# K loads two heads ahead of V instead of three, and one output turn ahead of the last values, in a decode attention kernel

## The chip, the cores and the metric

The kernel runs on one core of a Trainium2 chip. The metric is the device time of one execution in microseconds (us). Each comparison takes executions of both kernels on the same chip, in rounds; all runs of this study were in the fast state. A program on one core can only be called slow against its own fastest run, and none was more than 1.5% above that. Executions of one kernel still differ by up to 1.5%, and part of what follows is about why. Of the experiments, e1 to e4 ran on one chip and e5 to e12 on another; the kernel before was run beside each, with medians of 211.78 us (e1 to e4), 211.69 us (e5 to e8) and 211.52 us (e9 to e12).

## The reference, cut to what matters

One decode step: attention of 4 rows over the last 2048 positions of a K and V cache with 16 K/V heads (two query heads each), plus a mixing step and an MLP on the same input. The code is shortened.

```python
W = min(4096, max(256, Sk // 4))                    # 2048
q = (x @ wq) ...                                    # 32 query heads of 128
k = jnp.repeat(k_cache[:, :, Sk - W:, :], rep, axis=1)
v = jnp.repeat(v_cache[:, :, Sk - W:, :], rep, axis=1)
p = softmax(einsum("bhqd,bhkd->bhqk", q, k) * Dh ** -0.5)
A = einsum("bhqk,bhkd->bhqd", p, v) ... @ wo
# B: x1 + gelu(layernorm(x1) @ w3) @ w4, with x1 = x + mixer(...)
out = x + A + B          # A and B both get xn = layernorm(x)
```

Per head that is 2 MB of K and 2 MB of V; with the weights 87.17 MB are read.

## The kernel before: the parts that matter

Loads are issued in program order by SyncE, into a pool of six K/V tiles; a load waits until a tile has been freed.

```python
kvp = ctx.enter_context(tc.tile_pool(name="kv", bufs=NKV))        # NKV = 6
...
order = [("K", 0), ("K", 1), ("K", 2)]
for h in range(Hkv):
    order.append(("V", h))
    if h + 3 < Hkv:
        order.append(("K", h + 3))
...                       # w4, in six pieces, comes after the last K/V tile
```

The main loop has one turn per head. In turn t TensorE does the scores of head t and the values of head t-2, in four steps; VectorE transposes the K tile of head t in four pieces, one step ahead, and does the softmax maxima of head t-1 between them. A turn with a number (turn 15) is such a pass of the loop; "head 14's turn", "the moved turn" and `o_turn` mean something else, the transposes that turn the output of a head.

```python
for t in range(Hkv):
    hm, hv, hf, hp = t - 1, t - 2, t - 3, t - 4
    for s in range(NSL):
        ...
        n = t * NSL + s + 1
        if n < Hkv * NSL:
            k_transpose(*divmod(n, NSL))     # VectorE, needs the K tile
        if s == 0:
            if hm >= 0:
                sm_max(hm)                   # VectorE: max of the scores, then dm
            ...
        elif s == 1 and hm >= 0:
            sm_maxT(hm)                      # TensorE, needs dm ("the max matmul", mg)
        ...
        if hv >= 0:
            pv(hv, s)                        # TensorE, needs the V tile
        k_scores(t, s)                       # TensorE, needs the transposed K
        ...
```

After the loop comes the drain: the softmax of head 15, the values of heads 14 and 15, the turn of their outputs (four transposes on TensorE), then the w4 matmuls and the last projection.

```python
sm_exp(hl)                 # hl = 15, on ScalarE
...
sm_turn(hl); sm_den(hl); sm_rec(hl)
o_scale(hl - 1)            # ScalarE
for s in range(NSL):
    pv(hl, s)              # 16 value matmuls of head 15
o_scale(hl)                # ScalarE
o_turn(hl - 1); o_sum(hl - 1)
...
o_turn(hl); o_sum(hl); o_spread(hl); o_pick(hl)
mlp_out(*pieces[0])        # first w4 matmuls
o_proj(hl)
mlp_out(*pieces[1]) ...    # up to the pieces that land last
```

Of the kernel before, what the change touches and what calls it, by code (L numbers as in the profile page):

```python
# [22 lines left out]
def kernel(  # L23
# [17 lines left out]
    _, Hkv, Sk, Dh = A_k_cache.shape  # L41
# [337 lines left out]
    def sm_rec(h):  # L379
        rd = small.tile([P, 1], F32, tag="rd", bufs=4)  # L380
        nc.vector.reciprocal(out=rd[:], in_=st.pop(("dn", h))[:])
        st["rd", h] = rd

    def pv(h, s):
        if s == 0:
            O_ps[h] = ps_o.tile([P, NSL, Dh], F32, tag="O", name="O")
        vn = kv_tiles["V", h][:].rearrange("p (s c) d -> p s c d", s=NSL)
        for g in range(NQD):
            c = s * NQD + g
            nc.tensor.matmul(out=O_ps[h][g * QD:(g + 1) * QD], lhsT=PT[h][:, c, :], rhs=vn[:, :, c, :],  # L390
                             start=(s == 0), stop=False, skip_group_check=True)
        if s == NSL - 1:
            PT.pop(h)

    def o_scale(h):
        O_sb[h] = bigp.tile([P, NSL, Dh], F32, tag="big", name="O_sb")
        nc.scalar.activation(out=O_sb[h][:], in_=O_ps.pop(h)[:], func=ACT.Copy, scale=st.pop(("rd", h))[:, 0:1])  # L397

    def o_turn(h):
        oT = ps_m.tile([P, NSL, P], F32, tag="m", name="oT")  # L400
        o = O_sb.pop(h)
        for s in range(NSL):
            nc.tensor.transpose(out=oT[:, s, :], in_=o[:, s, :], identity=ident_w[:, s * NJ:s * NJ + P])  # L403
        st["oT", h] = oT

    def o_sum(h):
        oT = st.pop(("oT", h))
        v = oT[:].rearrange("p s (g x) -> p (s g) x", g=NQD)[:, :, 0:NJ].rearrange("p g (b r) -> p b r g", r=rep)
        k = h % WOQ
        if k == 0:  # L410
            st["on"] = small.tile([P, WOH, B], BF16, tag="on", name="on")
        with nc.allow_low_precision("summed in float32"):
            nc.vector.reduce_sum(out=st["on"][:, k * rep:(k + 1) * rep, :].rearrange("p r b -> p b r"),  # L413
                                 in_=v, axis=AX.X)
# [73 lines left out]
            acc_matmuls([(gT[:, u, :], w4[:, u, :]) for u in range(i, min(i + 2, hi))])  # L488


    order = [("K", 0), ("K", 1), ("K", 2)]
    for h in range(Hkv):
        order.append(("V", h))
        if h + 3 < Hkv:
            order.append(("K", h + 3))
    W3_AFTER = ("V", 2)
    pos = {"n": 0, "free": NKV}

# [70 lines left out]
    hl = Hkv - 1  # L569
# [14 lines left out]
    sm_den(hl)  # L584
    sm_rec(hl)
    o_scale(hl - 1)
    for s in range(NSL):
        pv(hl, s)
    o_scale(hl)
    o_turn(hl - 1)  # L590
    o_sum(hl - 1)
    pieces = list(zip(W4_PIECES, W4_PIECES[1:]))
    acc_odd = ps_acc.tile([P, CW], F32, tag="g", name="acc_odd")
    second += [acc_odd, True]
# [50 lines left out]
```

## Time and profile before

| | before |
|---|---|
| median of 3 runs | 211.63 us (211.63 to 212.5) |
| span in the profile | 209.8 us |
| read | 87.17 MB, 97.5% of 16 DMA engines' time |
| TensorE, VectorE busy | 71%, 57% |
| TensorE's waits for V | 37.1 us, ten times |

In the views PE is TensorE, PEld its weight loads, DVE VectorE, ACT ScalarE and SP SyncE. Of the tiles, kn and vn are K and V as loaded, kt the transposed K, S the scores, mg the max matmul's result, O the values, O_sb the scaled output and oT the turned one.

TensorE's waits for V are one line in the list of waits (engine and line, releaser: us in total, times, longest):

```profile
PE O L390 <- DMA vn<-in_A_v_cache_dram: 37.1, 10, 14.0
```

The rows of 40 slices tell which engine is never free: the DMA row is at 9 nearly throughout, TensorE's is not. The prediction below shows those lines. One row that it does not show matters later, TensorE's granted clock, the share of its full speed that it was allowed, in tenths (page of the kernel before):

```profile
PEclk9999589696969556958999979997999985969999
```

Here the reader sees that the clock falls to about half in single slices all over the run, also in the slice that covers 183.6 to 188.8 us (the 36th, a 6).

### The profile page before, as it was taken

To read this page: it belongs to the slowest core of one execution; us is meant where nothing else is said; L and a number is where in the kernel's file an instruction comes from. 1 tells how busy PE (TensorE), PEld (TensorE's weight loads), DVE (VectorE), ACT (ScalarE), POOL (GpSimd) and SP (SyncE) were. 2 spreads that over 40 slices of the span, in tenths; PEclk is the share of its full clock that TensorE was granted. 3 is DMA by queue.
4 is the path that set the end of the run, shared out by engine and by line. 5 is a ranking of instruction groups with operands and counts; after the bars stand their busy time and mean duration, and the time that the engine had idled before them with its cause. 6 is when DMAs were issued, how large, how long until landed. Compare 5 with 4: busy or idle time off the path is not lost.

```text
span 209.8 us, 2403 instructions
## 1 busy us (share of the span) xinstructions
PE 149.9 (71%) x955; PEld 62.8 (30%) x955; DVE 120.4 (57%) x217; ACT 33.9 (16%) x64; POOL 2.8 (1%) x15
## 2 busy tenths in 40 slices
PE   0287496869694009659899599977994926989884
PEld 0133132223231003214364143332532401425362
DVE  3741899584831082816706869995299471771421
ACT  7602201020211000202102121120111110202300
POOL 4010000000000000000000000000000000000000
PEclk9999589696969556958999979997999985969999
DMA  7999999999999999999999999999999999999991
GB/s 301 400 412 437 428 428 428 436 422 428 469 408 420 433 428 427 438 431 428 431 437 428 422 425 446 425 425 436 422 436 428 421 435 440 425 425 448 418 402 72
DMA packets 6659, 87.32 MB, mean 416 GB/s; under 512 B 748, under 2 KB 1016, under 8 KB 1656
## 3 DMA queue, kind: packets, MB, share of 16 engines
q1 hardware_dynamic: 6640, 87.17, 97.5%
q8 instruction: 7, 0.11, 0.2%
q14 instruction: 4, 0.03, 0.0%
q10 hardware_dynamic: 8, 0.00, 0.0%
HBM read 87.17 MB, written 0.00 MB: 415 GB/s over the span
## 4 chain that ended last, share of the span: by engine, by line
DMA 72%; PE 18%; DVE 6%; ACT 1%; issue 1%; SPq 0%; DVEq 0%
DMA vn<-in_A_v_cache_dram 35%; DMA w_sb<-in_B_w_dram 31%; PE S L338 7%; DMA wq_sb<-in_A_wq_dram 6%; DVE kt L225 3%; PE acc L183 2%; PE g_ps L456 2%; PE q_ps L285 2%; PE O L390 2%; PE oT L403 1%; DVE qz L317 1%; PE gT_ps L468 1%; DVE mx L344 1%; PE S L360 1%; ACT q_sb L296 1%
## 5 line engine op out<-in xcount | busy, mean ns | idle before, releaser
L225 DVE STREAM_TRANSPOSE kt<-kn 128x1024 int32<-128x1024 int32 x64 | 76.4, 1217 | 10.9 <-DMA kn<-in_A_k_cache_dram 10.6
L338 PE MATMUL S<-kt,qz 128*128 128x512 bf16 x256 | 79.7, 441 | 3.1 <-DVE kt L225 3.1
L390 PE MATMUL O<-vn,PT 128*32 128x512 bf16 x256 | 27.4, 426 | 38.9 <-DMA vn<-in_A_v_cache_dram 37.1
L338 PEld LDWEIGHTS <-qz 128*128 128x128 bf16 x256 | 21.7, 104 | 41.5 <-issue 25.8
L366 ACT ACTIVATE E<-S 128x512 bf16<-128x512 f32 x16 | 9.5, 597 | 122.6 <-PE S L360 122.6
L390 PEld LDWEIGHTS <-PT 128*32 128x32 bf16 x256 | 7.2, 94 | 47.3 <-issue 30.2
L372 DVE STREAM_TRANSPOSE PT<-E 128x512 bf16<-128x512 bf16 x16 | 11.4, 710 | 14.9 <-ACT E L366 14.9
L356 DVE TENSOR_REDUCE nm<-mg 8x1 bf16<-8x16 f32 x16 | 2.4, 152 | 20.7 <-PE mg L351 20.7
L397 ACT ACTIVATE O_sb<-O,rd 128x512 f32<-128x512 f32 x16 | 11.0, 686 | 15.6 <-issue 11.0
L413 DVE TENSOR_REDUCE on<-oT 128x8 bf16<-128x128 f32 x16 | 4.5, 280 | 12.7 <-PE oT L403 12.7
L403 PE MATMUL oT<-ident_w,O_sb 128*128 128x128 f32 x64 | 11.1, 302 | 0.3 <-ACT O_sb L397 0.3
L344 DVE TENSOR_REDUCE mx<-S 128x1 f32<-128x512 f32 x16 | 10.5, 657 | 1.3 <-PE S L338 1.3
L403 PEld LDWEIGHTS oT<-ident_w,O_sb 128*128 128x128 f32 x64 | 9.2, 161 | 5.3 <-issue 2.9
L183 PE MATMUL acc<-wo_sb,op 128*8 128x288 bf16 x56 | 7.5, 286 | 0.0
L376 PEld LDWEIGHTS dn<-rs,same_j 128*128 128x128 f32 x32 | 5.8, 188 | 2.9 <-ACT E L366 0.7
L360 PE MATMUL S<-nm,j_row 8*128 8x512 bf16 x16 | 6.5, 409 | 0.0
L329 PE MATMUL S<-negbig,ohT 4*128 4x512 bf16 x16 | 6.2, 385 | 0.0
L351 PE MATMUL mg<-dm,sel_jb 128*8 128x16 bf16 x16 | 2.8, 175 | 3.7 <-DVE dm L346 3.5
L183 PEld LDWEIGHTS <-op 128*8 128x8 bf16 x64 | 4.7, 87 | 2.2 <-issue 0.5
L351 PEld LDWEIGHTS <-sel_jb 128*8 128x8 bf16 x16 | 1.3, 83 | 13.1 <-DVE dm L346 6.5
L183 PE MATMUL acc<-w_sb,gT 128*8 128x288 bf16 x38 | 5.2, 286 | 0.1
L474 DVE COPY g_x<-gT_ps 128x64 f32<-128x64 f32 (+1 forms) x3 | 0.6, 195 | 7.7 <-PE gT_ps L468 7.7
(93 smaller groups left out, 84.3 us busy)
## 6 DMA issues: line engine op xcount, KB each, us to landing
kn<-in_A_k_cache_dram SPq DMA_DIRECT2D x16, 2048.0 KB, 21.9
vn<-in_A_v_cache_dram SPq DMA_DIRECT2D x16, 2048.0 KB, 24.4
wo_sb<-in_A_wo_dram SPq DMA_DIRECT2D x4, 1152.0 KB, 24.5
w_sb<-in_B_w_dram SPq DMA_DIRECT2D x1, 4608.0 KB, 34.3
wq_sb<-in_A_wq_dram SPq DMA_DIRECT2D x1, 4096.0 KB, 12.8
w_sb<-in_B_w_dram SPq DMA_DIRECT2D x1, 2592.0 KB, 31.9
w_sb<-in_B_w_dram SPq DMA_DIRECT2D x2, 864.0 KB, 33.9
w_sb<-in_B_w_dram SPq DMA_DIRECT2D x2, 576.0 KB, 33.0
```

The source lines that it names most:

```text
L183: nc.tensor.matmul(out=to[q:q + OR, :], lhsT=lhsT[:, NI - 1 - i:NI - 1 - i + OR], rhs=rhs[:, i * CW:(i + 1) * CW], start=start, stop=False ...
L225: nc.vector.transpose(out=kt[:], in_=src)
L329: nc.tensor.matmul(out=S_ps[h][:].rearrange("p (c k) -> p c k", k=QD), lhsT=ohT[:], rhs=negbig[:].unsqueeze(1).to_broadcast([B, SC, QD]), ...
L338: nc.tensor.matmul(out=S_ps[h][:], lhsT=qz[:, z0:z0 + P], rhs=kt[:, ib, :, e:2 * QD:2].rearrange("p c k -> p (c k)"), start=False, stop=Fa ...
L344: nc.vector.reduce_max(out=mx[:], in_=S_ps[h][:], axis=AX.X)
L360: nc.tensor.matmul(out=S_ps[h][:], lhsT=j_row[:], rhs=st.pop(("nm", h))[:, 0:1].to_broadcast([NJ, NW]), start=False, stop=False, skip_grou ...
L366: nc.scalar.activation(out=E[h][:].rearrange("p c k -> p (c k)"), in_=S_ps.pop(h)[:], func=ACT.Exp, scale=scale, accum_out=rs[:])
L372: nc.vector.transpose(out=PT[h][:], in_=E.pop(h)[:])
L376: nc.tensor.matmul(out=dn[:], lhsT=same_j[:], rhs=st.pop(("rs", h))[:], start=True, stop=True)
L390: nc.tensor.matmul(out=O_ps[h][g * QD:(g + 1) * QD], lhsT=PT[h][:, c, :], rhs=vn[:, :, c, :], start=(s == 0), stop=False, skip_group_check ...
L397: nc.scalar.activation(out=O_sb[h][:], in_=O_ps.pop(h)[:], func=ACT.Copy, scale=st.pop(("rd", h))[:, 0:1])
L403: nc.tensor.transpose(out=oT[:, s, :], in_=o[:, s, :], identity=ident_w[:, s * NJ:s * NJ + P])
```

## The change

The intent of the change is to have V tiles sooner (TensorE waits for them ten times) and to have head 14's output turned before TensorE goes on to head 15.

```diff
-    order = [("K", 0), ("K", 1), ("K", 2)]
+    order = [("K", 0), ("K", 1)]
     for h in range(Hkv):
         order.append(("V", h))
-        if h + 3 < Hkv:
-            order.append(("K", h + 3))
+        if h + 2 < Hkv:
+            order.append(("K", h + 2))
...
     o_scale(hl - 1)
+    o_turn(hl - 1)
+    o_sum(hl - 1)
     for s in range(NSL):
         pv(hl, s)
     o_scale(hl)
-    o_turn(hl - 1)
-    o_sum(hl - 1)
```

## The prediction

> **What bounds the kernel now.** I read the page's slices first, then the table of DMA queues, the chain of waits that ended last, and last the timeline of the final 30 us. The slices and the first queue of the kernel before:
>
> ```profile
> DMA  7999999999999999999999999999999999999991
> GB/s 301 400 412 437 428 428 428 436 422 428 469 408 420 433 428 427 438 431 428 431 437 428 422 425 446 425 425 436 422 436 428 421 435 440 425 425 448 418 402 72
> q1 hardware_dynamic: 6640, 87.17, 97.5%
> ```
>
> The DMA engines are full from the second slice of 5.2 us to the last but one. 87.17 MB at about 428 GB/s is 203.7 us of a span of 209.8 us. So the kernel is bound by its stream, and the order of the loads can matter only if the stream runs dry, or if work is left when the last byte has landed. The end of the chain of waits (start us, us, what):
>
> ```profile
> 174.94 31.06 DMA w_sb<-in_B_w_dram
> 206.00 0.04 issue
> 206.04 0.28 PE acc L183
> ```
>
> The chain ends on the pieces of w4, the last loads; 3.8 us after 206.00 the span is over. But TensorE had been busy right before: its matmuls of the earlier pieces end at about 205.75 (the last pair starts at 205.66), and the next start at 206.04, an idle time of 0.29 us. That is all the slack between the compute and the stream at the end. Whatever delays TensorE's last stretch by more than 0.3 us delays the end.
>
> Where that stretch starts is head 15's turn, and then the drain. From the timeline (start us, us, engine, line, what):
>
> ```profile
> 183.51 0.65 DVE L344 TENSOR_REDUCE mx<-S 128x1 f32<-128x512 f32 x1
> ...
> 184.65 0.57 PE L390 MATMUL O<-vn,PT 128*32 128x512 bf16 x4 [1.55 <-DMA vn<-in_A_v_cache_dram]
> ...
> 185.15 1.89 PE L338 MATMUL S<-kt,qz 128*128 128x512 bf16 x4
> ...
> 186.97 0.18 PE L351 MATMUL mg<-dm,sel_jb 128*8 128x16 bf16 x1
> ...
> 197.57 0.69 ACT L397 ACTIVATE O_sb<-O,rd 128x512 f32<-128x512 f32 x1 [0.45 <-ACT E L366]
> ...
> 197.92 1.05 PE L390 MATMUL O<-vn,PT 128*32 128x512 bf16 x16
> ...
> 198.90 0.66 PE L403 MATMUL oT<-ident_w,O_sb 128*128 128x128 f32 x4
> ...
> 199.07 0.69 ACT L397 ACTIVATE O_sb<-O,rd 128x512 f32<-128x512 f32 x1 [0.82 <-PE O L390]
> ...
> 199.81 0.66 PE L403 MATMUL oT<-ident_w,O_sb 128*128 128x128 f32 x4 [0.26 <-ACT O_sb L397]
> ```
>
> Turn 15 (scores of head 15, values of head 13) begins when V13 lands at 184.65. K15 had landed before it: by the view of the K tiles' issues it was issued at 157.1 and took 22.7 us, so it came at 179.8. The line at 197.92 is head 15's values, the two at 198.90 and 199.81 are the turns of the outputs of heads 14 and 15.
>
> **What the Trainium skill says.** "HBM Reference", Specifications, gives about 425 GB/s to a core that streams alone, bounded by its 16 DMA engines; the trace agrees, 428 in most slices. "DMA: Bandwidth & Descriptors", Anatomy of one DMA, says that the DMA engines wait for no semaphore, the issuing sequencer does: so what counts is that SyncE issues in time. "TensorE: Matmul & The Clock Gate", Architectural detail, says that VectorE and ScalarE are strict first-in-first-out: a transpose that waits for a K tile holds back all that stands behind it. No row of the trace before proves that by itself, but the order of VectorE's rows is the program's. The same page, Part 1, says that TensorE runs at half rate after an idle window: four score matmuls take 1.89 us at 185.15 after a wait and 1.07 us later.
>
> **The change part by part.** No byte and no arithmetic instruction is added or removed: the comparison of the instruction lists shows VectorE, ScalarE and GpSimd the same, TensorE with one group of four transposes (L403) moved ahead of the 16 value matmuls of head 15, and SyncE with K and V loads swapped pairwise.
>
> First, issue times. Six tiles are held, and a load takes the buffer that is freed first. In each turn t that is K_t's (its last transpose, mid-turn), then V_(t-2)'s (its last value matmul, at the end). Before, K_(t+3) took the first and V_(t+1) the second; now the other way round. All tiles are 2 MB, so each position in the stream is issued at about the same moment as before. The stream's reserve:
>
> ```profile
> DMA to landing us min/median/max: 14.0/21.9/36.4
> ```
>
> Of the 14.0 us of the worst K tile (issued at 111.45), 4.9 us are its own bytes (2.097 MB at 428 GB/s), so some 9 us of other loads were queued ahead of it. A shift of a turn by 1 to 2 us leaves the stream full. **So the stream still ends at about 206.0.**
>
> Second, what a turn waits for. Turn t needs K_0..K_t and V_0..V_(t-2). The set is the same, but its last member was V_(t-2) and is now K_t, at the same position, hence at the same time. Behind a V tile TensorE starts at once, with two K transposes already done; behind a K tile it first needs transposes. How VectorE goes on from a late K tile, the trace shows once, at 74.18:
>
> ```profile
> 74.18 2.37 DVE L225 STREAM_TRANSPOSE kt<-kn 128x1024 int32<-128x1024 int32 x2 [10.64 <-DMA kn<-in_A_k_cache_dram]
> 76.48 0.65 DVE L344 TENSOR_REDUCE mx<-S 128x1 f32<-128x512 f32 x1
> 77.17 0.23 DVE L346 TENSOR_SCALAR dm<-sel_g,mx 128x16 bf16<-128x16 bf16 x1
> ```
>
> From landing to dm done it is 77.40 - 74.18 = 3.2 us. TensorE's matmul of L351 needs dm and stands in front of the rest of the turn. With K15 at 184.65 instead of V13 it can run at 184.65 + 3.2 + 0.1 = 187.95, against 186.97 before: **+1.0 us**. The first scores start at 184.65 + 1.25 = 185.9 and end by 187.8 even at the half rate, so they don't set it; the later transposes (1.22 us each) keep ahead of the scores, since the projection of heads 8 to 11 takes 2.1 us of this turn on TensorE. In the other turns the same microsecond is absorbed: a turn runs about 7.7 us from its landing (174.92 to 182.6), about 9 us then, against 9.8 us for two tiles. Only turn 15 has nothing after it to wait for: what follows, the softmax of head 15, is one serial chain from 194.5 to 197.92, and V14 and V15 (landing at about 189.5 and 194.4, worked out at 4.9 us per tile from 184.65) are in both orders there in time.
>
> Third, the moved turn. Head 14's turn needs its scaled output, which ScalarE ends at 197.57 + 0.69 = 198.26, because it stands behind head 15's exponential. Head 15's values can start at 197.92. Before, they filled that wait, and head 14's turn in its turn filled the wait for head 15's scaled output (198.97 to 199.76). Now TensorE waits until 198.3, turns head 14 (0.59 us from its start to the next instruction, as at 196.26 to 196.85), and starts head 15's values at 198.9: **+1.0 us**. After them nothing fills the wait for the scaling.
>
> Sum: 1.0 + 1.0 = 2.0 us later at the first w4 matmul (201.13 becomes 203.1), less the slack of 0.3 us: the end comes 1.7 us later, 211.63 + 1.7 = **213.3 us**. All of w4 has then landed before TensorE gets to its last pieces, and the 4.6 us from the first w4 matmul to the last pieces are pure TensorE time.
>
> **Rivals.** (a) The end stays with the stream: 211.6 us. For it speaks that DMA has 97.5% and the chain ends on w4; against it the 0.29 us of slack. It would be true if turn 15 lost nothing (K15 landing earlier than V13 did) and the moved turn were hidden. (b) The K gate lengthens every turn past 9.8 us, VectorE becomes the pace (4 transposes of 1.22 us and some 2.5 us of softmax work in series after each landing), issues come late and the stream runs dry: 215 us or more. For it speaks that turns 7 to 10 already run with TensorE nearly full (19.65 of 20 us between 120 and 140); against it the 9 us of reserve, and that in that stretch no load is waited for, so the gate is not felt. (c) An earlier V removes the wait for V (37.1 us on TensorE in ten waits) and the kernel gets faster. The wait is removed in name only: it becomes a wait for K, and no wait in mid-stream moves the end of a full stream. That leaves no way below about 211.3 us. (d) Only one of the two parts costs: 212.3 us.
>
> **Range and chances.** Both microseconds come from single places of one trace; the clock gate can shift the short softmax chain by half a microsecond either way, and the three runs before spread by 0.9 us. I take 212.0 to 214.7, from rival (d) less a little to 1.4 us above my sum. Faster by over 2% (under 207.4) is against the stream; slower by over 2% (over 215.9) needs rival (b). So within 2% gets nearly all.
>
> **What would show it.** In the profile after: DMA still full in all slices, and the last w4 piece landed at about 206; the largest waits of TensorE for V gone, and in their place VectorE's waits for K, ten or so, at about the same times; L351 of turn 15 near 188.0; head 15's 16 value matmuls starting about a microsecond after the end of head 15's turned exponential; first w4 matmul near 203.1, last pieces with no wait for DMA, the span near 211.5. A dip in the DMA row before the end would make me wrong on the high side; a TensorE that still waits for w4 at the end, on the low side.

## The result, and the profile after

The changed kernel took 213.07 us (median of 6 runs, 212.69 to 214.27), the kernel before 211.63 (6 runs, 211.54 to 212.5). The ratio is 1.0069, with a 95% interval of 1.004 to 1.0097. Ratios here are the mean time of one kernel's fast runs over that of the other's of the same rounds, so not quite the ratio of the medians.

The page of the changed kernel, the rows of clock and DMA:

```profile
PEclk9999579696695579958999979997699996799999
DMA  7999999999999999999999999999999999999990
```

The stream is still full to the end, and the clock row has no dip in the last five slices. Then the list of waits:

```profile
DVE kt L225 <- DMA kn<-in_A_k_cache_dram: 38.5, 11, 13.2
PE S L338 <- DVE kt L225: 33.5, 11, 11.8
PEld L351 <- DVE dm L346: 13.2, 11, 3.1
```

TensorE's 37.1 us of waiting for V have become 38.5 us in which VectorE waits for K, and 33.5 us in which TensorE waits behind VectorE. Nothing was gained by the earlier V. The timeline of turn 15 and the drain, with the lines that answer to those in the prediction:

```profile
184.52 2.37 DVE L225 STREAM_TRANSPOSE kt<-kn 128x1024 int32<-128x1024 int32 x2 [1.15 <-DMA kn<-in_A_k_cache_dram]
...
185.82 1.06 PE L338 MATMUL S<-kt,qz 128*128 128x512 bf16 x4
...
187.86 0.17 PE L351 MATMUL mg<-dm,sel_jb 128*8 128x16 bf16 x1 [0.97 <-DVE rd L381]
...
197.95 0.69 ACT L397 ACTIVATE O_sb<-O,rd 128x512 f32<-128x512 f32 x1 [0.45 <-ACT E L366]
...
198.69 0.66 PE L403 MATMUL oT<-ident_w,O_sb 128*128 128x128 f32 x4 [0.53 <-ACT O_sb L397]
...
199.28 1.05 PE L390 MATMUL O<-vn,PT 128*32 128x512 bf16 x16
...
201.17 0.66 PE L403 MATMUL oT<-ident_w,O_sb 128*128 128x128 f32 x4 [0.84 <-ACT O_sb L397]
```

K15 landed at 184.5, where V13 had landed before. The max matmul (L351) is at 187.86, 0.89 us later than before. Head 15's values start at 199.28, 1.36 us later. The first w4 matmul is at 202.49 (201.13 before), and from there TensorE does not wait for w4 any more. The span grew by 1.1 us, to 210.9 us. The prediction had the max matmul at 188.0, the first w4 matmul at 203.1 and the span at 211.5: the signs it named came, the last two 0.6 us earlier than it said.

One thing does not fit the prediction. The first four scores of turn 15 took 1.06 us (185.82), before they took 1.89. The changed kernel ran this turn at the full clock, the kernel before had run it at the half. So the two profiles are not alike in a thing that the change did not touch, and differences between them mix the change with the clock.

### The profile page after: what moved, and what is told of

The parts are those of the page before. It is cut to its first block, busy times and chain, and to the rows that moved or that the text cites. A ratio compares the mean times of both kernels' runs of the same rounds, so it can differ in the third digit from the quotient of the medians.

```text
span 210.9 us, 2402 instructions
## 1 busy us (share of the span) xinstructions
PE 152.7 (72%) x955; PEld 64.5 (31%) x955; DVE 120.1 (57%) x217; ACT 33.9 (16%) x64; POOL 2.8 (1%) x15
## 4 chain that ended last, share of the span: by engine, by line
DMA 53%; PE 29%; DVE 12%; issue 3%; ACT 2%; SPq 0%; DVEq 0%; ACTq 0%
DMA kn<-in_A_k_cache_dram 46%; PE S L338 10%; DVE kt L225 7%; DMA wq_sb<-in_A_wq_dram 6%; PE acc L183 6%; PE O L390 3%; PE oT L403 3%; PE g_ps L456 2%; DVE mx L344 2%; PE q_ps L285 2%; PE S L360 1%; DVE dm L346 1%; ACT O_sb L397 1%; DVE qz L317 1%; PE gT_ps L468 1%
## 5 line engine op out<-in xcount | busy, mean ns | idle before, releaser
L338 PE MATMUL S<-kt,qz 128*128 128x512 bf16 x256 | 79.6, 441 | 33.7 <-DVE kt L225 33.5
L225 DVE STREAM_TRANSPOSE kt<-kn 128x1024 int32<-128x1024 int32 x64 | 76.7, 1223 | 39.1 <-DMA kn<-in_A_k_cache_dram 38.5
L338 PEld LDWEIGHTS <-qz 128*128 128x128 bf16 x256 | 22.7, 104 | 71.4 <-issue 55.6
L403 PE MATMUL oT<-ident_w,O_sb 128*128 128x128 f32 x64 | 12.1, 322 | 1.4 <-ACT O_sb L397 1.4
L403 PEld LDWEIGHTS oT<-ident_w,O_sb 128*128 128x128 f32 x64 | 9.8, 170 | 6.7 <-issue 3.2
L390 PEld LDWEIGHTS <-PT 128*32 128x32 bf16 x256 | 6.6, 94 | 11.5 <-issue 10.9
L351 PE MATMUL mg<-dm,sel_jb 128*8 128x16 bf16 x16 | 2.8, 173 | 9.5 <-DVE dm L346 7.3
L183 PE MATMUL acc<-wo_sb,op 128*8 128x288 bf16 x56 | 8.7, 313 | 0.0
L360 PE MATMUL S<-nm,j_row 8*128 8x512 bf16 x16 | 7.0, 437 | 0.0
L351 PEld LDWEIGHTS <-sel_jb 128*8 128x8 bf16 x16 | 1.3, 83 | 15.6 <-DVE dm L346 13.2
L456 PE MATMUL g_ps<-w_sb,ln2T 128*32 128x512 bf16 (+1 forms) x50 | 4.9, 444 | 0.0
L285 PE MATMUL q_ps<-wq_sb,xnT 128*32 128x512 bf16 x40 | 4.5, 631 | 0.2 <-DMA wq_sb<-in_A_wq_dram 0.2
```

The lines of the kernel that those rows point to most:

```text
L183: nc.tensor.matmul(out=to[q:q + OR, :], lhsT=lhsT[:, NI - 1 - i:NI - 1 - i + OR], rhs=rhs[:, i * CW:(i + 1) * CW], start=start, stop=False ...
L225: nc.vector.transpose(out=kt[:], in_=src)
L285: nc.tensor.matmul(out=q_ps[r][g * QD:(g + 1) * QD, :], lhsT=xnT[:, k, :], rhs=wq_sb[:, col:col + NW], start=(j == 0), stop=False, skip_gr ...
L338: nc.tensor.matmul(out=S_ps[h][:], lhsT=qz[:, z0:z0 + P], rhs=kt[:, ib, :, e:2 * QD:2].rearrange("p c k -> p (c k)"), start=False, stop=Fa ...
L360: nc.tensor.matmul(out=S_ps[h][:], lhsT=j_row[:], rhs=st.pop(("nm", h))[:, 0:1].to_broadcast([NJ, NW]), start=False, stop=False, skip_grou ...
L390: nc.tensor.matmul(out=O_ps[h][g * QD:(g + 1) * QD], lhsT=PT[h][:, c, :], rhs=vn[:, :, c, :], start=(s == 0), stop=False, skip_group_check ...
```

## The experiments

The theory at the start was that of the prediction: two delays of TensorE's last stretch, and a small slack to the stream.

### The two parts alone

```diff
 # e1_order_only, from the changed kernel: the new order; the drain as before
+    for s in range(NSL):
+        pv(hl, s)
+    o_scale(hl)
     o_turn(hl - 1)
     o_sum(hl - 1)
-    for s in range(NSL):
-        pv(hl, s)
-    o_scale(hl)
```

> The new load order alone; head 14's turn stays behind head 15's values. Theory (two separate delays of TensorE's last stretch, with 0.29 us of slack to the stream): the trace after showed head 15's values 1.36 us late, of which 0.98 is the moved turn, so 0.4 us here (start near 198.3), most of it taken by the slack: 211.6 to 212.2 us, ratio 1.000 to 1.003, TensorE waiting for w4 at the end for at most 0.1 us. The prediction on record would have +0.7 (1.0 less 0.3): 212.3. Rival (every turn's wait for K costs, in sum most of the 1.44 us): 212.6 or more.

Measured: 212.29 us (six runs), ratio 1.002 (0.9993 to 1.0048). The runs fall in two groups: 211.70, 211.73, 211.84 and 212.73, 213.20, 213.32. Neither figure of the expectation describes this. The profiled run belongs to the second group (213.20 us) and offers a reason; of the first group there is no trace. The table of stretches (us, then busy us of TensorE, weight load, VectorE, ScalarE, GpSimd, then granted clock, DMA share, GB/s):

```profile
184.20:187.60 3.40, 1.96 (x18) 0.80 (x16) 3.06 (x4) 0.00 (x0) 0.00 (x0) 1.00 1.00 429
187.60:191.00 3.40, 3.16 (x13) 1.41 (x12) 3.27 (x7) 0.00 (x0) 0.00 (x0) 0.50 1.03 443
```

After 3.4 us in which TensorE was busy for 1.96 us, its clock was halved for the next 3.4 us.

```diff
 # e2_turn_only: the old order; the drain of the changed kernel
     o_scale(hl - 1)
+    o_turn(hl - 1)
+    o_sum(hl - 1)
     for s in range(NSL):
         pv(hl, s)
     o_scale(hl)
-    o_turn(hl - 1)
-    o_sum(hl - 1)
```

> The moved turn alone, in the old load order. Theory: head 15's values start 1.0 us after their start in the kernel before, relative to head 15's exponential (0.2 to 0.5 us of waiting for the scaled output of head 14, then 0.59 us of transposes); less the slack of 0.29 that is +0.7: 212.3 us, ratio 1.002 to 1.005. Rival (four transposes moved between two places of one engine cost nothing, the order of the loads does it all): 211.6, ratio 1.000.

Measured: 211.67 us, ratio 1.0014 (0.9973 to 1.0056), five runs at 211.5 to 211.9 and one at 214.63. The time is the rival's (211.6 us), the mechanism the theory's. In the trace the moved turn waits for ScalarE as predicted, but turn 15 ran at full clock:

```profile
185.05 1.08 PE L338 MATMUL S<-kt,qz 128*128 128x512 bf16 x4
...
186.06 0.17 PE L351 MATMUL mg<-dm,sel_jb 128*8 128x16 bf16 x1
...
196.90 0.66 PE L403 MATMUL oT<-ident_w,O_sb 128*128 128x128 f32 x4 [0.53 <-ACT O_sb L397]
...
197.48 1.05 PE L390 MATMUL O<-vn,PT 128*32 128x512 bf16 x16
```

V13 landed at 184.72, as before. Yet the max matmul is 0.91 us sooner than in the profile of the kernel before, and head 15's values start 0.44 us sooner in spite of the moved turn. The moved turn delays head 15's values by 0.98 us (in the changed kernel they start at 199.28 instead of 198.30, which is 0.35 us after the start of head 14's scaling, as before). So the half-rate window in the profile of the kernel before had cost that run about 0.98 + 0.44 = 1.4 us in turn 15, and its slack of 0.29 us was that of a run at half rate. The new theory: **at full clock the kernel before has some 1.7 us of slack, and half-rate windows of TensorE's clock decide how much of it is left.** ("Warm" in the expectations below means at full clock.)

### Which turn's wait counts

```diff
 # e3_mid_order_turn: the changed kernel, K15 back ahead of V13
+    i15 = order.index(("K", Hkv - 1))
+    order[i15 - 1], order[i15] = order[i15], order[i15 - 1]
 # e4_last_order_turn: the old order, V13 put ahead of K15; moved turn
+    i15 = order.index(("K", Hkv - 1))
+    order[i15], order[i15 + 1] = order[i15 + 1], order[i15]
```

> The changed kernel with only K15 put back ahead of V13: turns 2 to 14 wait for K, turn 15 waits for V13 again. Theory (only turn 15's wait reaches the end): as the moved turn alone, 212.3 us, about 0.4 below the changed kernel. Rival (the waits of all turns add up): as the changed kernel, 213.0.

> The old load order with only V13 put ahead of K15, and the moved turn: turns up to 14 wait for V as before, turn 15 waits for K15. Theory: as the changed kernel, 212.7 to 213.1 us; turn 15's first max matmul about 3.3 us after K15's landing. Rival (mid-stream waits do it): as the moved turn alone, 212.3.

Measured: e3 211.86 us, ratio 1.0011 (0.9984 to 1.0037); e4 215.4 us, ratio 1.017 (1.0152 to 1.0188), all four runs between 215.32 and 215.64. With the wait for K in turns 2 to 14 and not in turn 15, e3 is like the moved turn alone (e2): the waits in mid-stream do not count. That half of the theory holds. But e4, with only the last wait changed, is 2.3 us slower than the changed kernel, which nobody had expected. Its stretches:

```profile
196.10:199.50 3.40, 2.48 (x22) 1.29 (x23) 1.54 (x7) 1.38 (x3) 0.00 (x0) 1.00 0.93 396
199.50:206.30 6.80, 5.57 (x48) 2.71 (x48) 1.43 (x4) 0.69 (x1) 0.00 (x0) 0.50 0.87 353
```

From 199.5 to 206.3 the clock is halved, through head 15's values, its turn and the first w4 matmuls. A second window, 185.8 to 189.2, lies in turn 15. In the timeline the 16 value matmuls take 1.90 us instead of 1.05.

### The clock as the suspect: keeping TensorE busy

Matmuls of a constant into a PSUM tile that nobody reads are put where TensorE waits. They change no result and need only the bank that is free at that time.

```diff
+    def keep_busy(k):
+        if not junk:
+            junk.append(ps_acc.tile([P, NW], F32, tag="g", name="junk"))
+        for _ in range(WARM[k]):
+            nc.tensor.matmul(out=junk[0][:], lhsT=ident_bf[:], rhs=qz[:, 0:NW], start=True, stop=True)
...        # turn 15: ahead of the first scores and of the max matmul
...        # drain: after pv(14, 0), after the denominator, after head 15's values
```

> The kernel of the run before (old order, V13 ahead of K15, moved turn: 215.4 us in four of four) with 17 matmuls into an unread PSUM tile, put where TensorE waits in turn 15 and in the drain (7 before head 15's first scores, 3 before the max matmul, 2, 2 and 3 in the drain). Theory (the 2.3 us over the changed kernel are half-rate windows of TensorE's clock, 185.8 to 189.2 and 199.5 to 206.3 in its trace, not a cost of the order): no half-rate window after 186, and 212.8 to 213.2 us. Rival (the late V13/K15 swap itself delays the stream or the chain): stays above 214.5, and a little above 215.4 for the added matmuls.

> The changed kernel with 11 such matmuls (1, 3, 2, 2, 3). Theory: its profiled run had no half-rate window after 182.3 and took 212.69; so all runs come to 212.5 to 212.9, and the 213.0 to 214.3 of the others go away. Rival (the spread is from the stream): median 213.1 and spread as before, or up by the 11 matmuls (11 x 0.22 us = 2.4 us if they were not hidden).

> The new order alone with 9 such matmuls (3, 3, 2, 1, 0). Its runs without them fell in two groups, 211.7 to 211.8 and 212.7 to 213.3; the profiled one (213.2) had a half-rate window from 187.6 to 191.0. Theory (order alone, warm: head 15's values at 198.3, the slack of the warm kernel before is 1.7 us and holds the order's 1.8): all runs 211.5 to 211.9. Rival (the order alone costs half a microsecond whatever the clock): 212.2.

Measured, with the kernel before at 211.69 us in the same rounds:

| kernel | plain | kept busy |
|---|---|---|
| V13 ahead of K15, moved turn (e4, e5) | 215.4 (215.32 to 215.64) | 212.66 (212.63 to 212.79) |
| the changed kernel (first result, e6) | 213.07 (212.69 to 214.27) | 212.82 (212.66 to 212.99), ratio 1.0052 (1.0039 to 1.0065) |
| the new order alone (e1, e7) | 212.29 (211.70 to 213.32) | 211.89 (211.80 to 212.31), ratio 1.0008 (0.9994 to 1.0022) |

The changed kernel's plain runs are of other rounds, and e1 and e4 of another chip, on which the kernel before took 211.78 us; e4's ratio to it falls from 1.017 to 1.0046. More work on TensorE makes each of them faster or steadier, e4 by 2.7 us. The rivals (the swap itself, the stream, a cost of the order whatever the clock) fall. e5 and e6 end within 0.2 us of each other, so the changed kernel's loss from the order is all in turn 15. In e5's trace no half-rate window lies after 186. Between e7 and e6 stands the moved turn, on runs with no slack left (e7's trace has no wait for w4): 212.82 - 211.89 = 0.93 us, near the predicted 1.0. The two differ in their added matmuls too (3, 3, 2, 1, 0 against 1, 3, 2, 2, 3), but the traces show the same cost: from K15's landing to the matmuls just ahead of w4's it is 16.74 us in e7 (185.07 to 201.81) and 17.69 us in e6 (184.44 to 202.13).

Two runs of e7, 212.07 and 212.31, lie above the 211.9 that was expected. The second is the profiled one, in which K15 landed at 185.07, about 0.6 us later than in the traces of e5 and e6 (184.49, 184.44). So a part of the spread that is left comes from the stream; of the other runs there is no trace.

### Measuring the slack

```diff
 # the kernel before; 4 matmuls ahead of turn 15's first values, 2 in the drain
+    WARM = {"turn 15": 4, "drain": 2, "delay": 6}      # 14 in the second
...
     o_turn(hl - 1)
     o_sum(hl - 1)
+    keep_busy("delay")
     ...
     o_turn(hl)
```

> Measures the slack of the kernel before: 6 matmuls hidden in waits (4 in front of turn 15, 2 in the drain) to keep the clock at full rate, and 6 more (6 x 0.213 = 1.28 us, of which 0.3 fill a wait) on TensorE's path just ahead of head 15's turn. Theory (slack of a warm kernel before 1.7 us: 0.29 read in the profile plus 1.4 that its half-rate window in turn 15 had cost): the delay of 1.0 vanishes, 211.5 to 211.8. Rival (slack 0.29, as the prediction had it): 1.0 - 0.3 later, 212.3.

> The same with 14 matmuls in the path, a delay of 14 x 0.213 - 0.3 = 2.7 us. Theory (slack 1.7): 1.0 later than before, 212.6, about the changed kernel's time. Rival (slack 0.29): 2.4 later, 214.0. Both theories fall if it stays at 211.6.

Measured, with the kernel before at 211.52 us: the short delay 211.56, ratio 1.0002 (0.9989 to 1.0015); the long one 212.62, ratio 1.0044 (1.003 to 1.0058). How long the delays were is in the timelines, from the start of head 15's values to head 15's turn, in e9 and in e10:

```profile
196.71 1.05 PE L390 MATMUL O<-vn,PT 128*32 128x512 bf16 x16
...
199.48 0.60 PE L403 MATMUL oT<-ident_w,O_sb 128*128 128x128 f32 x4
```

```profile
197.27 1.05 PE L390 MATMUL O<-vn,PT 128*32 128x512 bf16 x16
...
201.76 0.60 PE L403 MATMUL oT<-ident_w,O_sb 128*128 128x128 f32 x4
```

That is 2.77 and 4.49 us, against 1.89 us in the kernel before (197.92 to 199.81). A delay of 0.9 us disappears, one of 2.6 us costs 1.1. So the slack is about 1.5 us, not 0.29. The list of waits of e9 between 196 and 206 us still has a wait for w4, which with the delay makes 1.3 us in that run:

```profile
PE acc L183 <- DMA w_sb<-in_B_w_dram: 0.4, 1, 0.4
```

### The place of the turn, and an attempt at a faster kernel

```diff
 # e8_after_turn_mid, from the changed kernel
-    o_turn(hl - 1)
-    o_sum(hl - 1)
     for s in range(NSL):
+        if s == NSL // 2:
+            o_turn(hl - 1)
+            o_sum(hl - 1)
         pv(hl, s)
```

> The changed kernel with head 14's turn between the two halves of head 15's values, so that eight value matmuls fill the wait for head 14's scaled output, while the four transposes still stand ahead of the scaling of head 15. Theory (of the moved turn's 0.98 us, 0.4 are the wait and 0.59 the transposes): 0.4 us under the changed kernel, 212.3 to 212.9, with no wait for ScalarE ahead of head 14's transposes. Rival (only the place of the wait changes): 213.0.

> Head 14's turn between the halves of head 15's values again, now with 9 hidden matmuls that keep the clock at full rate (the run without them was in half-rate windows in five of six executions, 213.9 to 214.2, and 212.57 in the sixth). Theory: 0.4 us below the changed kernel kept busy in the same way (212.82), 212.3 to 212.5. Rival (place of the turn doesn't matter): 212.8.

Measured: e8 213.95 us, ratio 1.0098 (1.0075 to 1.0121), slower than the changed kernel and outside what was expected. Five runs are at 213.9 to 214.2, one at 212.57; the profiled one had a half-rate window in turn 15, well ahead of the edit. Kept busy (e11) it took 212.52 us (212.42 to 212.66), ratio 1.0046 (1.0033 to 1.0059). Against the changed kernel kept busy that is 0.3 us less by the medians, but those are from different rounds and the ratios to the kernel before, 1.0046 and 1.0052, have overlapping intervals. In e11's trace the first eight value matmuls do start before head 14's turn, at 198.41, and all 16 are over by 200.16 (200.33 in the changed kernel, in which K15 had landed 0.1 us sooner). From K15's landing that is 15.54 us against 15.81 us, a gain of 0.27 us. I take the direction as shown by the trace; the total time does not resolve the size.

```diff
 # e12_before_busy_pieces: the kernel before, kept busy (4 and 2)
-    W4_PIECES = [0, NFH, NF - 12, NF - 6, NF - 2, NF - 1, NF]
+    W4_PIECES = [0, NFH, NF - 12, NF - 4, NF - 2, NF - 1, NF]
```

> An attempt at a faster kernel: the kernel before with the 6 hidden matmuls, and the fourth piece of w4 cut from four rows to two (the third grows from six to eight), so that only four matmuls of the odd sum, not eight, wait for its landing. Theory (with the slack of 1.7 us TensorE waits for the stream, and 4 pairs less behind the last but two landings are 0.2 us): 211.3 to 211.5, no run above 212. Rival (the last two rows' landing sets the end): 211.6.

Measured: 211.65 us (211.41 to 211.92), ratio 1.0005 (0.9992 to 1.0017): no gain, above the 211.3 to 211.5 that was expected. Its list of waits after 195 us gives the slack a second time, now as waits for w4 in a run without delay:

```profile
PE acc L183 <- DMA w_sb<-in_B_w_dram: 1.5, 2, 0.8
```

TensorE waits twice, together for 1.5 us: once for the first piece of w4 and once for a later one.

```profile
200.65 0.28 PE L183 MATMUL acc<-w_sb,gT 128*8 128x288 bf16 x1 [0.81 <-DMA w_sb<-in_B_w_dram]
...
205.46 0.28 PE L183 MATMUL acc<-w_sb,gT 128*8 128x288 bf16 x1 [0.73 <-DMA w_sb<-in_B_w_dram]
```

No version in this study beats the kernel before; with 1.5 us of slack in TensorE's work, that one is held by its stream. The kernel before with the matmuls in its waits and nothing else changed was not run; e9 and e12 stand for it.

## Why the prediction was right, point by point

**The stream sets the end unless TensorE is late.** Right: the DMA row stands at 8 or 9 in every trace until the last two slices (428 GB/s in the kernel before is the median of its slices, not the value of most), and a change of K and V order in mid-stream (e3) costs nothing that the runs resolve.

**Turn 15 loses by waiting for K instead of V.** Right in mechanism, too small in size. The predicted 1.0 us came from 187.95 against 186.97, and the 186.97 was read in a turn at half rate. At full clock the max matmul stands 1.34 us behind the start of head 13's values when V gates (186.06 - 184.72 in e2; 1.33 to 1.34 in e9 and e12). Behind K15's transposes it stands 3.34 us (187.86 - 184.52 in the changed kernel, 3.34 in e7). For landings at the same time the term is thus 3.34 - 1.34 = 2.0 us; with the landings of these two traces it is 187.86 - 186.06 = 1.8 us. The line at 185.15 in the prediction shows the half rate, four scores in 1.89 us instead of 1.07, and the prediction says so; it did not carry that into its subtraction. The lines of e7:

```profile
185.07 2.37 DVE L225 STREAM_TRANSPOSE kt<-kn 128x1024 int32<-128x1024 int32 x2 [1.38 <-DMA kn<-in_A_k_cache_dram]
...
188.41 0.17 PE L351 MATMUL mg<-dm,sel_jb 128*8 128x16 bf16 x1 [0.31 <-DVE rd L381]
```

**The moved turn costs 1.0 us.** Right: 0.93 us between e6 and e7 by time, 0.95 us by their traces. In the traces head 14's turn waits 0.53 us for ScalarE and its transposes take 0.59 us ahead of the values.

**The slack is 0.29 us.** This step failed. It took one profile's idle time as a property of the kernel. That run had a half-rate window in turn 15; e9, e10 and e12 give 1.3 to 1.5 us. The 0.29 us is also the gap between weight loads (PEld), not between matmuls: by the timeline the last earlier matmul ends at 205.67 + 0.29 = 205.96, which leaves 0.08 us to 206.04. Beside 1.5 us neither reading matters.

**The sum.** The prediction had 1.0 + 1.0 - 0.3 = 1.7 us. The runs kept at full clock have 1.8 to 2.0 + 0.93 - 1.5 = 1.2 to 1.4 us, against 212.82 - 211.69 = 1.13 us measured. The 0.93 comes from e6 itself, so the test without it is e7, the order alone: 1.8 to 2.0 less 1.5 is 0.3 to 0.5 us, against 0.20 us measured (-0.1 to 0.5 by its ratio). The terms close to within 0.3 us.

The errors in the turn-15 term and in the slack had one source, the half-rate window in the profile of the kernel before. Up to the max matmul it took 0.98 us (186.97 - 184.65 - 1.34). That made the turn-15 term too small and the slack too small by the same amount, and so cancels. From there to head 15's values it took another 0.50 us (10.95 us, in e12 10.45). That is missing in the slack alone and made the sum too high. That 213.3 came so close to 213.07 is in part luck: the plain runs of the changed kernel lie between 212.69 and 214.27, those kept busy between 212.66 and 212.99, and half-rate windows would explain the difference of 0.25 us between the medians. Its one profiled run, of 212.69 us, had none after 182.3, and the intervals of the two ratios (1.0069 and 1.0052) overlap, so this is argued and not shown. The kernel before hides such a window: its profiled run had one in turn 15 and took 211.62 us.

**The rivals.** (a), the stream alone, is what each part alone does at or near full clock (medians e2 211.67, e7 211.89). Only together they go clearly past the slack, so (d), half the cost from one part, was wrong too: each part alone costs nearly nothing. (b) did not occur in any run. (c) is refuted by the waits: 37.1 us for V became 38.5 us for K.

What stays open is why a half-rate window falls here or there. In e4 it came after a stretch with 2.48 of 3.4 us busy (196.1 to 199.5), while e2 kept the full clock after 2.12 of 3.5 us (196.1 to 199.6). A count over the 14 traces says more. In each of them the clock changes only on a grid of 3.41 us. I cut each trace on its grid, from its first clock record (at 17 to 20 us) to 205 us. Of the stretches at full clock, all in which TensorE was busy for less than 1.6 us were followed by one at half clock (92 of 92), and none of those with 2.5 us or more (0 of 366). In between it went either way (28 of 76), and there busy time alone does not decide it. The plain runs without a profile do not tell where their windows lay.

## What to carry to other kernels

Here the stream of loads was full, and the order within it moved only the last stretch of compute. In such a kernel look there, and ask of each candidate for "last to land" how much serial work stands between its landing and the engine that ends the kernel. Read slack from more than one execution, or with a delay put in on purpose, and compare the granted clock of the two stretches before you subtract their times. Where TensorE waits often and its tail is on the path, a few harmless matmuls in the waits can tell a cost of the change from a cost of the clock.

## What the Trainium skill lacked or had wrong

- "TensorE: Matmul & The Clock Gate", Part 1, has the half rate follow an idle window of about 3.4 us, and its "A second HAM failure mode" names micro-idles between groups as a second way. Here half rate followed stretches in which TensorE was busy for 1.96 of 3.4 us (e1) and 2.48 of 3.4 us (e4), with single waits of about 1 us or less between. The page gives no measure of how busy is busy enough; the count above gives one for these traces: always half rate after less than 1.6 us, never after 2.5 us or more, open between.
- The same page tells modelers that the ramp at the start costs under 1% of a typical span. It gives no figure for windows that come back on a serial tail: in e4 they cost 2.7 us of 215.4, 1.3%, and its four runs lay within 0.32 us.
- For a kernel with gaps the same page, in "HAM oscillation", proposes longer runs of matmuls or padding. Matmuls put into the waits (17 in e5) are not among these and took the 2.7 us away.
- No page says that the place of these windows makes the slack of a kernel vary from run to run: 0.29 us in one profile, about 1.5 us measured.
